# Windowed attention into a gated feed-forward on one core: w_in's casts shared with ScalarE, and units 4 to 15 at other places in the order

## The chip, the core and the metric

The kernel runs on one core of one Trainium2 chip. The core has a matrix engine (TensorE, PE in the profile), VectorE (DVE), ScalarE (ACT), GpSimd (Pool, POOL) and a sync engine (SyncE, SP) that here only issues transfers. Each engine runs its own list of instructions in order, and they wait for each other by semaphores. Data come from HBM by DMA into SBUF; matmuls write to PSUM, of which this kernel uses all eight banks. The metric is the time of one execution on the device in microseconds (us). Three runs of the kernel before took 225.61, 227.72 and 227.89 us, a median of 227.72.

## The reference

q, k and v have 4 batches, 8 heads, 768 positions and 64 columns. A position attends to itself, the 127 before it and the first four positions ("sinks"). The outputs of the heads side by side are x, 3072 tokens by 512, and x goes through two matrix products with a gate between them.

```python
scores = q @ k.T / sqrt(64)                    # kept where key < 4 or 0 <= query - key < 128
x = softmax(scores) @ v                        # per head; heads joined: 3072 x 512
h = x @ w_in                                   # 512 x 2048
g = h * (1 / (1 + exp(-beta * h)))
out = g @ w_out                                # 2048 x 512, float32
```

## The kernel before

**Units and tiles.** The attention is done in 32 units. Unit n is one pair of heads (n % 4) of one batch (n // 8) and one half of the sequence, 384 positions (n // 4 % 2). Four units fill one tile T = n // 4 of 384 tokens of xT, the transposed x in bf16, one of four products' depth (c, 0 to 3) each. For T there are 16 tiles of h (128 columns of w_in by 384 tokens): tile i is T = i // 16, m = i % 16. Each is four matmuls (c = 0 to 3, `hidden_matmul`), a tanh on ScalarE (`tanh`, line 755) and the gate on VectorE (`gate`, line 769), which multiplies the tanh plus one by h in place of the logistic function (the 0.5 goes into the output copy, beta is halved) and leaves g in bf16. Then 3 x 16 projections of g against w_out per T (`project`, line 796) accumulate the output rows, which ScalarE or VectorE copies out.

**A unit's steps** are named "in", "sink", "a", "b", "av" and "out". "in" (`transpose_in`, line 513) turns q and k with six 128-column transposes on TensorE into one PSUM bank, and one copy (line 522) takes them to qkT. "a" and "b" (`scores`, line 569) are two chunks of scores with an exponential on ScalarE after each (line 576); then VectorE multiplies the result by a 0/1 mask (`mask`, line 587). For units in ADDED (n < 6) the mask is put in otherwise: two 384-column matmuls by the identity (line 561) add a large negative number to the masked scores in PSUM first, and the VectorE product is left out. "sink" is the score against the four sink keys, for units of the second half only (units 4 to 7 among these). "av" (`attend`, line 696) multiplies by v, `normalise` divides by the sum (lines 705 and 707), and "out" (`transpose_out`, line 724) turns the result into xT, with a copy at line 728. From unit 12 on the transposes are done by DMA, and two chunks go as one.

**Loads and casts.** All inputs arrive in float32. `load(n)` fetches q, k and v of a unit (590 KB), `load_w(i)` one of eight pieces of w_in (i < 8) or of w_out (512 KB each), all on SyncE's queue in the order of the calls. Piece i of w_in holds 512 of its columns and two of the four depths: tiles m = 0 to 3 need pieces 0 and 1, m = 4 to 7 pieces 2 and 3, m = 8 to 11 pieces 4 and 5, m = 12 to 15 pieces 6 and 7; the even piece serves c = 0 and 1, the odd one c = 2 and 3. Pool casts each piece to bf16 (`cast_w`, line 478, 128 x 1024), and q, k and v of each unit (`cast`, lines 490 and 493), into three buffers for q and k that units take in turn.

**PSUM.** `six` is six banks: s0, s1, tr and av (scores, transposes, attention output) and h0 and h1. Two more are acc0 and acc1. Tiles 0 to 3 use acc0, acc1, h1 and h0; tiles 4 to 15 only acc0 and acc1 in turn; tiles 16 to 31 all four; later tiles others. Before the first tile is gated, TensorE is also given matmuls on constants (`keep_busy`).

**The order.** The body writes operations down by slots s. Slot s = 0 to 31 holds tile i = s; 32 to 47 the projections of T = 0; from 48 on tile s - 16 with the projections of the T before. EARLY gives units 4 to 7 their slots by step, as fractions between tiles; FIRST gives units 8 to 31 their slot of "in", with "sink", "a", "b", "av", "out" 1, 2, 3, 5 and 7 slots later. BANK_B and BANK_S choose the PSUM banks of units 4 to 7. `loads` and `casts` tie later loads and casts to slots. This is not yet the order of execution: `Prog.order` simulates the five engines and the DMA queues with the written costs (`busy`, `lag`; transfers by size over a rate) and places, engine by engine, whichever ready operation can start first within a window of 160. Its result is a fixed list for each engine, so an operation whose input arrives later than planned holds up those behind it.

Of the kernel before, what the change touches and what calls it, by code (L numbers as in the profile page):

```python
# [17 lines left out]
TT = 384  # L18
# [5 lines left out]
NW = 8  # L24
# [17 lines left out]

EARLY = {4: {'in': 0.2, 'sink': 3.0, 'a': 3.4, 'b': 5.0, 'av': 5.6, 'out': 8.0},
# [244 lines left out]
def bass_streamingllm_window__then__act_swish_beta_kernel(  # L288
# [187 lines left out]
    def cast_w(i):  # L476
        view, _, dst = w_piece(i)
        op("gp", lambda e: e.tensor_copy(dst, view), r=[("wst", i % NW)],  # L478
           w=[("w_in" if i < NW else "w_out", i % NW)], busy=985.0, lag=100.0)

    def cast(n, first=False):
        _, _, half, pb = place(n)
        z = n % NQK

        def view(name):
            return stage[name][pb][:, :, 3 * half:3 * half + 3, :].rearrange("p h c d -> p c h d")

        for x, name in enumerate("qk"):
            eng = "dve" if first and name == "k" else "gp"
            op(eng, lambda e, x=x, name=name: e.tensor_copy(qk16[z][:, x, :, :, :], view(name)),  # L490
               r=[(name + "_stage", pb, half, hh) for hh in range(2)], w=[(name + "16", z)],
               busy=451.0, lag=100.0)
        op("gp", lambda e: e.tensor_copy(v_aug[pb][:, 3 * half:3 * half + 3, :, 0:D], view("v")),  # L493
           r=[("v_stage", pb, half, hh) for hh in range(2)], w=[("v_aug", pb, half)], busy=451.0,
           lag=100.0)
# [56 lines left out]
    def scores(n, c, bank, name):  # L552
        _, _, half, pb = place(n)
        at = 0
        if n < ADDED:
            w = width(half, c)
# [7 lines left out]
        with P.together("pe"):  # L564
            for kb, qb, nq in CHUNKS[half][c]:
                w = 128 * nq
                for hh in range(2):
                    rows = slice(64 * hh, 64 * hh + 64)
                    op("pe", lambda e, at=at, w=w, kb=kb, qb=qb, hh=hh, rows=rows: e.matmul(  # L569
                        bank[:, hh, at:at + w], qkT[pb][rows, kb // 3, 1, kb % 3 * 128:kb % 3 * 128 + 128],  # L570
                        qkT[pb][rows, half, 0, qb % 3 * 128:qb % 3 * 128 + w], start=n >= ADDED,
                        stop=True, skip_group_check=n < ADDED),
                       r=[("qT", pb, half), ("qkT", pb, kb // 3)], w=[f"{name}{hh}"],
# [6 lines left out]
    def mask(n, c):  # L580
        if n < ADDED:
            return
# [161 lines left out]
    def hidden_matmul(i, c):  # L744
# [28 lines left out]
    def project_last(half, m):  # L773
# [4 lines left out]
                                           w_out16[:, m, cols], start=(m == 0), stop=(m == NM - 1)),  # L778
                  r=[("g", T % 2, m), ("w_out", m // 2)], w=[name], **pe(256))
        if m == NM - 1:  # L780
# [14 lines left out]
    def project(T, t, m, bank, name, eng="act"):  # L795
        node = op("pe", lambda e: e.matmul(bank, g[T % 2][:, m, t * 128:(t + 1) * 128],  # L796
                                    w_out16[:, m, :], start=(m == 0), stop=(m == NM - 1)),
           r=[("g", T % 2, m), ("w_out", m // 2)], w=[name], **pe(NOUT))
        if m == NM - 1:
# [33 lines left out]
    for hh in range(2):  # L833
# [15 lines left out]
    load_w(7)  # L849
# [66 lines left out]
    for s in sorted(slots):  # L916
# [14 lines left out]
        for n, step in here:  # L931
            half = place(n)[2]
            if step == "in" and n < XBAR:
                transpose_in(n, eng="dve")
            if step == "sink" and half == 1:
                scores_sink(n, *((h_ps[:, 0, :], "h0") if BANK_S.get(n) == "h" else (s_ps[:, 0, :], "s0") if n < PAIRED
                                 else (tr_ps, "tr")))
# [17 lines left out]
            if step == "out":  # L955
                if n < XBAR:
                    transpose_out(n, eng="act" if n < 8 else "dve")
        if s in casts:
# [102 lines left out]
```

## Time and profile before

| what | value |
|---|---|
| median of three runs | 227.72 us |
| the profiled execution | 226.35 us |
| its span, first to last instruction | 224.6 us |
| granted TensorE clock | 1.000 |
| TensorE busy | 216.6 us (96%) |
| ScalarE busy | 142.0 us |
| VectorE busy | 133.3 us |
| Pool busy | 75.2 us |
| first projection of T = 0 starts | 51.53 us |

The profile is of one execution; its own time is 1.75 us longer than its span. Times inside it count from the first instruction. A matmul row is counted from its start to its modelled end, and rows overlap, so a row's mean is longer than the distance between matmuls that follow each other. In rows of the order of time, "x8" says that eight instructions were merged, and brackets tell how long the engine had been idle and what ended that. In groups, the columns are the operation with its shapes, the count, busy time and mean ns of one, then idle time of the engine ahead of it.

### The profile page before, as it was taken

To read this page: it belongs to the slowest core of one execution; us is meant where nothing else is said; L and a number is where in the kernel's file an instruction comes from. 1 tells how busy PE (TensorE), PEld (TensorE's weight loads), DVE (VectorE), ACT (ScalarE), POOL (GpSimd) and SP (SyncE) were. 2 spreads that over 40 slices of the span, in tenths; PEclk is the share of its full clock that TensorE was granted. 3 is DMA by queue.
4 is the path that set the end of the run, shared out by engine and by line. 5 is a ranking of instruction groups with operands and counts; after the bars stand their busy time and mean duration, and the time that the engine had idled before them with its cause. 6 is when DMAs were issued, how large, how long until landed. Compare 5 with 4: busy or idle time off the path is not lost.

```text
span 224.6 us, 4507 instructions
## 1 busy us (share of the span) xinstructions
PE 216.6 (96%) x1732; PEld 122.5 (55%) x1753; DVE 133.3 (59%) x259; ACT 142.0 (63%) x222; POOL 75.2 (33%) x149
## 2 busy tenths in 40 slices
PE   7997999999999999999999999999999999999995
PEld 4463555655555555555465655555556565555554
DVE  5477787897766535555285566667667666254300
ACT  2674897794446666556587669566877584465410
POOL 6769569599335211444301623700000000000000
PEclk9999999999999999999999999999999999999999
DMA  6999999899999899999998999551021002111012
GB/s 186 292 330 287 270 339 288 270 392 278 142 206 221 241 229 167 277 260 190 235 238 184 227 223 182 146 136 32 32 85 64 20 9 72 50 47 47 22 74 95
DMA packets 95438, 39.80 MB, mean 177 GB/s; under 512 B 81960, under 2 KB 88376, under 8 KB 95416
## 3 DMA queue, kind: packets, MB, share of 16 engines
q1 hardware_dynamic: 93760, 38.75, 69.3%
q10 hardware_dynamic: 1656, 0.76, 1.2%
q8 instruction: 14, 0.23, 0.4%
q14 instruction: 8, 0.07, 0.1%
HBM read 27.30 MB, written 6.29 MB: 150 GB/s over the span
## 4 chain that ended last, share of the span: by engine, by line
PE 89%; DVE 4%; DMA 2%; ACT 1%; issue 1%; POOL 0%; ACTq 0%; DVEq 0%
PE acc L796 34%; PE six L747 30%; PE acc L747 6%; PE six L696 5%; PE six L642 3%; DMA v_stage<-in_v_dram 2%; PE six L569 2%; PE six L796 1%; PE six L513 1%; PE six L685 1%; PE six L542 1%; DVE g L769 1%; PE six L561 1%; DVE v_sink L891 1%; DVE qkT L522 1%
## 5 line engine op out<-in xcount | busy, mean ns | idle before, releaser
L796 PE MATMUL acc<-w_out,g 128*128 128x512 bf16 x332 | 84.4, 379 | 0.9
L755 ACT ACTIVATE th<-six,beta_half 128x384 f32<-128x384 f32 x106 | 61.1, 582 | 30.5 <-PE six L747 25.2
L747 PE MATMUL six<-xT,w_in 128*128 128x384 bf16 x424 | 78.1, 326 | 0.1
L769 DVE SCALAR_TENSOR_TENSOR g<-th,six 128x384 bf16<-128x384 f32 x106 | 57.2, 551 | 28.9 <-ACT th L755 25.9
L747 PEld LDWEIGHTS six<-xT,w_in 128*128 128x128 bf16 x424 | 40.4, 98 | 29.1 <-ACT E L613 0.7
L796 PEld LDWEIGHTS acc<-w_out,g 128*128 128x128 bf16 x352 | 32.9, 98 | 33.9 <-issue 1.8
L662 DVE TENSOR_TENSOR E<-E,mask_all 128x1536 bf16<-128x1536 bf16 x20 | 19.4, 972 | 30.1 <-ACT E L654 24.8
L654 ACT ACTIVATE E<-six 128x1536 bf16<-128x1536 f32 x16 | 22.3, 1448 | 10.6 <-PE six L642 10.6
L490 POOL CAST qk<-q_stage 128x384 bf16<-128x384 f32 x32 | 17.7, 554 | 29.8 <-DMA q_stage<-in_q_dram 17.0
L576 ACT ACTIVATE E<-six 128x768 bf16<-128x768 f32 x24 | 18.8, 810 | 9.3 <-PE six L569 9.3
L493 POOL CAST v_aug<-v_stage 128x384 bf16<-128x384 f32 x32 | 16.7, 532 | 16.2 <-DMA v_stage<-in_v_dram 9.6
L490 POOL CAST qk<-k_stage 128x384 bf16<-128x384 f32 x31 | 16.5, 532 | 16.3 <-DMA k_stage<-in_k_dram 16.2
L804 ACT ACTIVATE out_sb<-acc 128x512 f32<-128x512 f32 x22 | 12.9, 598 | 12.4 <-PE acc L796 12.2
L696 PEld LDWEIGHTS six<-v_aug,E 128*128 128x128 bf16 x384 | 17.0, 97 | 4.3 <-POOL v_aug L493 0.7
L696 PE MATMUL six<-v_aug,E 128*128 128x65 bf16 x384 | 18.9, 193 | 0.5 <-POOL v_aug L493 0.3
L707 DVE TENSOR_TENSOR o_norm<-six,rden 128x384 bf16<-128x384 f32 x32 | 17.8, 557 | 1.4
L747 PE MATMUL acc<-xT,w_in 128*128 128x384 bf16 x88 | 16.8, 327 | 1.2 <-DVE g L769 1.2
L755 ACT ACTIVATE th<-acc,beta_half 128x384 f32<-128x384 f32 x22 | 12.7, 583 | 5.6 <-PE acc L747 4.9
L769 DVE SCALAR_TENSOR_TENSOR g<-th,acc 128x384 bf16<-128x384 f32 x22 | 11.7, 551 | 3.7 <-ACT th L755 3.3
L747 PEld LDWEIGHTS acc<-xT,w_in 128*128 128x128 bf16 x88 | 7.9, 98 | 7.0 <-DVE g L769 2.1
L478 POOL CAST w_in<-wst 128x1024 bf16<-128x1024 f32 x8 | 9.0, 1129 | 6.1 <-DMA wst<-in_moe_w_in_dram 5.8
L522 DVE COPY qkT<-six 128x768 bf16<-128x768 bf16 (+1 forms) x10 | 9.1, 913 | 2.4 <-PE six L513 2.4
(72 smaller groups left out, 156.7 us busy)
## 6 DMA issues: line engine op xcount, KB each, us to landing
out_dram<-out_sb SPq DMA_DIRECT2D x23, 256.0 KB, 2.6
wst<-in_moe_w_in_dram SPq DMA_DIRECT2D x8, 512.0 KB, 6.4
wst<-in_moe_w_out_dram SPq DMA_DIRECT2D x8, 512.0 KB, 7.7
q_stage<-in_q_dram SPq DMA_DIRECT2D x8, 384.0 KB, 4.2
k_stage<-in_k_dram SPq DMA_DIRECT2D x8, 384.0 KB, 3.9
v_stage<-in_v_dram SPq DMA_DIRECT2D x8, 384.0 KB, 4.0
v_stage<-in_v_dram SPq DMA_DIRECT2D x30, 96.0 KB, 3.9
q_stage<-in_q_dram SPq DMA_DIRECT2D x12, 192.0 KB, 5.0
```

The lines of the kernel that those rows point to most:

```text
L490: op(eng, lambda e, x=x, name=name: e.tensor_copy(qk16[z][:, x, :, :, :], view(name)), r=[(name + "_stage", pb, half, hh) for hh in range( ...
L493: op("gp", lambda e: e.tensor_copy(v_aug[pb][:, 3 * half:3 * half + 3, :, 0:D], view("v")), r=[("v_stage", pb, half, hh) for hh in range(2 ...
L576: op("act", lambda e: e.activation(E[n % 2][:, c, :, 0:at], bank[:, 0:2, 0:at], AF.Exp, bias=0.0, scale=SCALE), x=[f"{name}0", f"{name}1"] ...
L654: op("act", lambda e, u=u, first=first: e.activation(E[u % 2][:, :, :, :].rearrange("p c h x -> p (c h x)"), six[:, first:first + 3, :].re ...
L662: op("dve", lambda e: e.tensor_tensor(both, both, mask_all[:, half, :].unsqueeze(1).to_broadcast([128, 2, 768]), ALU.mult), r=[("E", z, 0) ...
L696: last=(x == len(kbs) - 1): e.matmul(av_ps[:, at + hh * D1:at + hh * D1 + D1], E[z][:, c, h2, col:col + 128], v_aug[pb][:, kb, hh, :], sta ...
L707: op("dve", lambda e: e.tensor_tensor(o_norm[o][:, :, :, :].rearrange("p m h d -> p (m h) d"), src[:, :, 0:D], rden[z][:, :].unsqueeze(2). ...
L747: return op("pe", lambda e: e.matmul(bank, w_in16[:, c, m * 128:(m + 1) * 128], xT[:, c, T * TT:(T + 1) * TT], start=(c == 0), stop=(c == 3)),
L755: op("act", lambda e: e.activation(th[i % 3][:, :], bank, AF.Tanh, bias=0.0, scale=beta_half[:, m:m + 1]), x=[name], r=["beta"], w=[("th", ...
L769: op("dve", lambda e: e.scalar_tensor_tensor(g[T % 2][:, m, :], th[i % 3][:, :], 1.0, bank, ALU.add, ALU.mult), r=[("th", i % 3)], x=[name ...
L796: node = op("pe", lambda e: e.matmul(bank, g[T % 2][:, m, t * 128:(t + 1) * 128], w_out16[:, m, :], start=(m == 0), stop=(m == NM - 1)), r ...
L804: op("act", lambda e: e.activation(out_sb[z][:, :], bank, AF.Copy, bias=0.0, scale=0.5), x=[name], w=[("out_sb", z)], **act(NOUT))
```

## The change

Five things change, all in the order and in who does which cast; what is computed is the same.

- `cast_w`: pieces 1, 2, 3 and 5 of w_in are cast in two halves, one depth by Pool and one by ScalarE (128 x 512 each). The tiles' products wait for their own depth (`w_in` has a third index).
- `hidden`: tiles 4 to 19 issue their four products as four separate operations, so that the planner can put other work between them or start one before the others' inputs are there.
- Loads: unit 4 is loaded after piece 0 and unit 5 after piece 2; unit 6 comes ahead of pieces 4 and 5, and unit 7 after them.
- The set ADDED: chunk a of unit 6 and chunk b of unit 7 take their mask by matmuls too; `mask` leaves VectorE's product out for them.
- Slots and engines of units 4 to 31: EARLY, FIRST, banks; ScalarE copies the transposes in for units 4 and 9 and out for units 6 and 7, VectorE the others of units 4 to 11 (before: VectorE all in, ScalarE out for units 4 to 7). Some written costs (985 to 1080 ns for a piece, 451 to 530 ns for a cast of q, k or v) and the slots of later loads change with them.

```diff
-EARLY = {4: {'in': 0.2, 'sink': 3.0, 'a': 3.4, 'b': 5.0, 'av': 5.6, 'out': 8.0},
-         5: {'in': 2.4, 'sink': 3.8, 'a': 3.8, 'b': 6.6, 'av': 6.8, 'out': 9.6},
-         6: {'in': 3.9, 'sink': 6.9, 'a': 7.0, 'b': 8.0, 'av': 14.7, 'out': 15.0},
-         7: {'in': 6.9, 'sink': 13.2, 'a': 13.2, 'b': 14.0, 'av': 14.8, 'out': 15.7}}
-BANK_B = {4: 'h', 5: 's', 6: 'h', 7: 's'}
-BANK_S = {4: 'h', 5: 'h', 6: 'h', 7: 'h'}
-
-FIRST = {8: 27, 9: 33, 10: 34, 11: 38}
-FIRST.update({12: 44, 13: 47, 14: 50, 15: 53, 16: 60, 17: 60})
-FIRST.update({n: 68 + 8 * (n // 2 - 9) for n in range(18, NU)})
+EARLY = {4: {'in': -3.3, 'sink': 3.1, 'a': -3.0, 'b': 1.5, 'av': 3.2, 'out': 5.8},
+         5: {'in': -0.7, 'sink': 5.1, 'a': 4.0, 'b': 5.7, 'av': 9.3, 'out': 13.3},
+         6: {'in': 3.3, 'sink': 8.0, 'a': 7.2, 'b': 8.5, 'av': 12.7, 'out': 14.6},
+         7: {'in': 5.6, 'sink': 12.0, 'a': 9.3, 'b': 12.5, 'av': 12.8, 'out': 15.4}}
+BANK_B = {4: 's', 5: 'h', 6: 'h', 7: 'h'}
+BANK_S = {4: 't', 5: 'h', 6: 'h', 7: 't'}
+
+TURN_IN = {4: 'act', 5: 'dve', 6: 'dve', 7: 'dve', 8: 'dve', 9: 'act', 10: 'dve', 11: 'dve'}
+TURN_OUT = {4: 'dve', 5: 'dve', 6: 'act', 7: 'act', 8: 'dve', 9: 'dve', 10: 'dve', 11: 'dve'}
+
+APART = 20
+
+HALVED = (1, 2, 3, 5)
+
+FIRST = {8: 17, 9: 23, 10: 27, 11: 28}
+FIRST.update({12: 39, 13: 43, 14: 46, 15: 50, 16: 60, 17: 60})
+FIRST.update({n: (68, 76, 83, 92, 99, 108, 116)[n // 2 - 9] for n in range(18, NU)})
...
-ADDED, FAR = 6, -float(1 << 20)
+ADDED = {*((n, c) for n in range(4) for c in range(2)), (4, 0), (4, 1), (5, 0), (5, 1), (6, 0), (7, 1)}
+FAR = -float(1 << 20)
...
     def cast_w(i):
         view, _, dst = w_piece(i)
+        name = "w_in" if i < NW else "w_out"
+        if i in HALVED:
+            n = 1
+            op("act", lambda e: e.copy(dst[:, n:], view[:, n:]), r=[("wst", i % NW)], w=[(name, i % NW, 1)],
+               **act(512))
+            op("gp", lambda e: e.tensor_copy(dst[:, 0:n], view[:, 0:n]), r=[("wst", i % NW)],
+               w=[(name, i % NW, 0)], busy=600.0, lag=100.0)
+            return
         op("gp", lambda e: e.tensor_copy(dst, view), r=[("wst", i % NW)],
-           w=[("w_in" if i < NW else "w_out", i % NW)], busy=985.0, lag=100.0)
+           w=[(name, i % NW, 0), (name, i % NW, 1)], busy=1080.0, lag=100.0)
...
-           r=[("w_in", m // 4 * 2 + c // 2), ("xT", T, c)], w=[name], **pe(TT))
+           r=[("w_in", m // 4 * 2 + c // 2, c % 2), ("xT", T, c)], w=[name], **pe(TT))
...
     def hidden(i):
-        with P.together("pe"):
-            for c in range(3 if i < 4 else 0, 4):
-                node = hidden_matmul(i, c)
+        for cs in ((3,),) if i < 4 else ((0,), (1,), (2,), (3,)) if i < APART else (range(4),):
+            with P.together("pe"):
+                for c in cs:
+                    node = hidden_matmul(i, c)
         tanh(i)
         return node
...
     load_w(0)
+    load(4)
     load_w(1)
     load_w(2)
+    load(5)
     load_w(3)
-    load(4)
-    load(5)
     load(6)
-    load(7)
     load_w(4)
     load_w(5)
+    load(7)
     load_w(6)
     load_w(7)
...
-    at = {16: 38, 17: 46, 18: 52, 19: 57, 24: 69, 25: 75, 26: 81, 27: 87}
+    at = {16: 38, 17: 44, 18: 50, 19: 55, 24: 70, 25: 76, 26: 84, 27: 89}
```

More of the change, by code (lines that the diff above doesn't have):

```diff
@@ L491, in cast @@
                r=[(name + "_stage", pb, half, hh) for hh in range(2)], w=[(name + "16", z)],
-               busy=451.0, lag=100.0)
+               busy=530.0, lag=100.0)
         op("gp", lambda e: e.tensor_copy(v_aug[pb][:, 3 * half:3 * half + 3, :, 0:D], view("v")),
-           r=[("v_stage", pb, half, hh) for hh in range(2)], w=[("v_aug", pb, half)], busy=451.0,
+           r=[("v_stage", pb, half, hh) for hh in range(2)], w=[("v_aug", pb, half)], busy=530.0,
            lag=100.0)
@@ L554, in scores @@
         at = 0
-        if n < ADDED:
+        if (n, c) in ADDED:
             w = width(half, c)
@@ L570, in scores @@
                         bank[:, hh, at:at + w], qkT[pb][rows, kb // 3, 1, kb % 3 * 128:kb % 3 * 128 + 128],
-                        qkT[pb][rows, half, 0, qb % 3 * 128:qb % 3 * 128 + w], start=n >= ADDED,
-                        stop=True, skip_group_check=n < ADDED),
+                        qkT[pb][rows, half, 0, qb % 3 * 128:qb % 3 * 128 + w], start=(n, c) not in ADDED,
+                        stop=True, skip_group_check=(n, c) in ADDED),
                        r=[("qT", pb, half), ("qkT", pb, kb // 3)], w=[f"{name}{hh}"],
@@ L580, in mask @@
     def mask(n, c):
-        if n < ADDED:
+        if (n, c) in ADDED:
             return
@@ L778, in project_last @@
                                            w_out16[:, m, cols], start=(m == 0), stop=(m == NM - 1)),
-                  r=[("g", T % 2, m), ("w_out", m // 2)], w=[name], **pe(256))
+                  r=[("g", T % 2, m), ("w_out", m // 2, m % 2)], w=[name], **pe(256))
         if m == NM - 1:
@@ L797, in project @@
                                     w_out16[:, m, :], start=(m == 0), stop=(m == NM - 1)),
-           r=[("g", T % 2, m), ("w_out", m // 2)], w=[name], **pe(NOUT))
+           r=[("g", T % 2, m), ("w_out", m // 2, m % 2)], w=[name], **pe(NOUT))
         if m == NM - 1:
@@ L933, in bass_streamingllm_window__then__act_swish_beta_kernel @@
             if step == "in" and n < XBAR:
-                transpose_in(n, eng="dve")
+                transpose_in(n, eng=TURN_IN.get(n, "dve"))
             if step == "sink" and half == 1:
-                scores_sink(n, *((h_ps[:, 0, :], "h0") if BANK_S.get(n) == "h" else (s_ps[:, 0, :], "s0") if n < PAIRED
+                scores_sink(n, *((h_ps[:, 0, :], "h0") if BANK_S.get(n) == "h" else (tr_ps, "tr") if BANK_S.get(n) == "t" else (s_ps[:, 0, :], "s0") if n < PAIRED
                                  else (tr_ps, "tr")))
@@ L956, in bass_streamingllm_window__then__act_swish_beta_kernel @@
                 if n < XBAR:
-                    transpose_out(n, eng="act" if n < 8 else "dve")
+                    transpose_out(n, eng=TURN_OUT.get(n, "dve"))
         if s in casts:
```

## The prediction, made before the changed kernel was run

> **What bounds the kernel now.** I read the page first, then the windows by stage, then the order of time where the windows show holes.
>
> ```profile
> span 224.6 us, 4507 instructions
> PE 216.6 (96%) x1732; PEld 122.5 (55%) x1753; DVE 133.3 (59%) x259; ACT 142.0 (63%) x222; POOL 75.2 (33%) x149
> DMA  6999999899999899999998999551021002111012
> ```
>
> TensorE is busy 96% of the span, and the DMA engines are full from 5 to about 150 us. The change lies in the first 70 us. Its stages, by the windows (after the times: length, then busy us and instructions of each engine, clock, DMA share, GB/s):
>
> ```profile
> 18.30:31.00 12.70, 11.01 (x121) 6.13 (x119) 9.63 (x18) 10.30 (x18) 9.03 (x17) 1.00 0.97 293
> 31.00:41.00 10.00, 9.60 (x88) 5.79 (x87) 7.74 (x16) 8.06 (x16) 7.21 (x12) 1.00 1.01 289
> 41.00:51.20 10.20, 10.20 (x81) 6.07 (x79) 9.61 (x18) 9.12 (x17) 9.08 (x14) 1.00 0.99 348
> 51.20:66.50 15.30, 15.05 (x134) 7.66 (x133) 10.82 (x23) 6.14 (x9) 8.90 (x17) 1.00 0.99 202
> 66.50:225.00 158.50, 154.46 (x1166) 87.25 (x1183) 84.59 (x158) 98.89 (x150) 28.49 (x59) 1.00 0.60 136
> ```
>
> Busy time flatters TensorE, since a lone matmul also counts its drain. So I price its work by rows of the chain that stand back to back: eight x @ w_in products (128x384) 1.30 us, three projections 0.65, twelve attention products 0.36, three transposes 0.17, a score chunk 0.27 and 0.11 for the change into it. Times the counts of the groups in each window this is 10.8 us of work in the 12.7 us from 18.3; 9.25 of 10.0; about 10.2 of 10.2; 14.9 of 15.3. So **TensorE loses 1.9 + 0.75 us between 18.3 and 41 us and nearly nothing from there to 66.5**. Before 18.3, from the first transposes at 4.5, it has about 11 us of work in 13.8. What makes the holes, in order of time (start, length, instruction, in brackets the idle time and what ended it):
>
> ```profile
> 28.96 1.04 POOL L478 CAST w_in<-wst 128x1024 bf16<-128x1024 f32 x1 [2.61 <-DMA wst<-in_moe_w_in_dram]
> 30.31 1.16 POOL L478 CAST w_in<-wst 128x1024 bf16<-128x1024 f32 x1 [0.31 <-DMA wst<-in_moe_w_in_dram]
> 31.52 0.76 PEld L747 LDWEIGHTS acc<-xT,w_in 128*128 128x128 bf16 x6 [0.38 <-POOL w_in L478]
> ...
> 33.77 1.04 POOL L478 CAST w_in<-wst 128x1024 bf16<-128x1024 f32 x1 [0.38 <-PE six L696]
> ```
>
> ```profile
> 37.21 1.21 DVE L769 SCALAR_TENSOR_TENSOR g<-th,acc 128x384 bf16<-128x384 f32 x2 [0.26 <-ACT th L755]
> 37.83 1.47 PE L747 MATMUL acc<-xT,w_in 128*128 128x384 bf16 x8 [0.40 <-DVE g L769]
> ```
>
> Pieces 4 and 5 of w_in land at 29 and 30.3 us, so tiles 8 and 9 wait until 31; between 25 and 31 no tile runs. From there the pairs of tiles, 10 and 11 to 14 and 15, follow at 33.59, 35.74 and 37.83: two accumulators, each held for product, tanh and gate, give a pair every 2.1 us, and TensorE waits for the gate.
>
> **The loads.** From w_in 0 (cast at 13.73) to w_in 7 (33.77) 20.0 us bring seven pieces (0.524 MB) and four units (0.590 MB): 301 GB/s, 1.74 us a piece, 1.96 a unit. Estimated by these, pieces 1 to 7 land at 15.4, 17.2, 18.9, 28.5, 30.3, 32.0, 33.7 before, within 0.5 us of their casts in the trace. The new order gives: unit 4 15.7, w1 17.4, w2 19.1, unit 5 21.1, w3 22.8, unit 6 24.8, w4 26.5, w5 28.3, unit 7 30.2, w6 32.0, w7 33.7. Unit 4 gains 5 us, pieces 4 and 5 gain 2, pieces 1 to 3 lose 2 to 4, unit 7 loses 3.4, the last piece is where it was: no byte is saved. Nothing else is passed on SP's queue; loads from unit 8 on stand behind the same bytes.
>
> **The halved casts.** Pool's half is taken as half of 1.04 = 0.52; ScalarE's, 512 columns, as 0.55 (its copy of 384 columns is 0.47, its 512-column out_sb is 0.60): a piece is ready 0.5 us sooner, Pool is spared 2.1 us, ScalarE gets 2.2. Bounds: nothing gained, to 0.5 us on each. The copies on ScalarE add waits for a landing; behind each are queued exponentials and tanhs.
>
> **Tiles product by product.** Tiles 4 to 19 issue the same matmuls; a tile can start on piece 2 while piece 3 is on its way, and tiles 18 and 19 on finished units while unit 7 is not. Cost at nothing: successive products load new weights anyway (98 ns under a 163 ns product).
>
> **Tiles, worked forward.** Tiles 4 and 5 start at 20.5 as before, but end at 24.0 with w3 (22.8 + 0.55 + two products of each) and not at 22.3. Gates end at 25.2 and 25.7, tiles 6 and 7 at 26.5, 8 and 9 with w5's cast (28.9) and 0.65 at 29.6, 10 and 11 at about 31.8, 12 and 13 with w7's (34.8) at 35.5, 14 and 15 start at 36.4. In the trace they start at 37.83: **1.4 us**. By then units 4 to 7 must be through too. Unit 7 lands at 30.2; its output came 12 us after its v landed (25.84 to 37.73) in queues, while its shortest chain, cast 1.5, transposes and copy 1.5, scores and exps 2, products, normalising and output 2, is 7: 37 us, just in time. Tiles 18 and 19 can have up to three of four products done by then (6 x 0.163 = 1.0). So 1.4 to 2.4 us; I take **2.3**, the holes being 2.65 and unit 4's early work also fitting in the hole before 18.3.
>
> **Masks as matmuls.** Chunks (6, a) and (7, b) get two more 384-column products each: 4 x 0.163 = 0.65 us of TensorE; VectorE loses two masks of 0.56 to 0.73. They lie in the holes of 25 to 34; without that cover they cost 0.65. I take **0.2**.
>
> **Units 8 to 15 earlier.** Unit 8 goes from tile 27 to 17, 9 from 33 to 23, 10 and 11 to 27 and 28; its data was cast by 36.5 in the trace and its transposes ran at 41.7, so it is ready. Nothing is saved; 4.0 us of TensorE work (a unit of these: transposes 0.34, scores 0.76, products 0.36, output 0.17) moves out of the projections of tile 0 into x @ w_in of tile 1. There it needs other engines: through tile 31 ScalarE gets six exps of 0.81, two copies of unit 4's and 9's transposes at about 0.81 (the exp has their shape), the halves 2.2, and loses two outputs of 0.47: 27.5 + 7.7 = 35.2 us. VectorE gets 5.7 on 27.0. TensorE's work to there is 30.5 + 4.65 = 35.2 us. **ScalarE has as much to do as TensorE**; in the same stage of the trace it was 89% and VectorE 94% busy. What relieves it: the exps of units 10 and 11 (3.2 us) may come after the last tanh, the projections leaving ScalarE idle 9 of 15.3 us. I take **0.3** lost; the bounds are 0 and rival 2's price. Units 12 to 15, loads 17 to 27: a few tiles, in stages where TensorE has no hole; 0, bounds 0.5 either way.
>
> The masks of units 8 to 11 move among w_out's casts on Pool. In the trace one such mask beside Pool's cast took 0.77 (at 49.70) and a free one 0.55. The Trainium skill (SBUF — State Buffer, Who interferes with whom) says that a VectorE instruction with two SBUF inputs and a GpSimd one that reads SBUF exclude each other for a whole instruction; by that each could wait out a cast of 1.04, eight of them 8 us of VectorE. The rows bear out a part of it, 0.2 each.
>
> **Sum:** -2.3 + 0.2 + 0.3 = -1.8, and 0.2 for Pool's relief between 15 and 25 us (4.87 and 4.56 of 5 busy there): -2.0. The profiled execution took 226.35 us, 1.75 more than its span; so **224.3**. The three runs shown have a median of 227.72, 1.4 above that execution, and spread over 1%; about 1% (2.3 us) is what a measurement of this kernel can tell from no change.
>
> **Rivals.**
> 1. *The whole of the holes is filled.* 2.65 and 1 us ahead of 18.3, units 12 to 15 another 0.5: 222.3. For it: unit 4 five us earlier. Against it: w7 as late as ever, and two accumulators.
> 2. *ScalarE becomes the bound in x @ w_in of tile 1: slower.* Place: from 18.3 to tile 31. If its 35.2 us run at the 89% of 41 to 51.2, tile 31 ends at 18.3 + 39.5 = 57.8; left then are 14.9 - 4.0 and the 0.4 lost in the stage, 11.3: 69.1 in place of 66.5, **229.0**. It decides when ScalarE can't keep 95% (36.9 us: 55.2 + 11.3 = 66.5). For it: VectorE's 32.7 us beside it. Against it: exps that may slide.
> 3. *The early gain is eaten.* A copy of w_in stands at ScalarE's head before its piece has landed. The planner counts 380 GB/s where 301 are had, so it can be wrong by a transfer, 1.74 us, with tanhs and exps behind it, whose banks TensorE waits for; or unit 7, 3.4 us later, takes the place of the weights. Either gives back 1.7: **226.1**. For it: tiles 4 and 5 do end later. Against: TensorE has units 4 to 6 meanwhile.
>
> **Chances:** the forecast 0.38 (223.3 to 225.3), rival 1 0.18, rival 3 0.22, rival 2 0.22. Of the forecast's case a little over half lies past 1%: faster 0.40, same 0.38, slower 0.22. The range takes rival 1 to 221.5 and rival 2 up to its price.
>
> **What would show it.** Right: w_in 4's first product by 28 us; tile 14's first product near 36.4; ScalarE's four 512-column copies of 0.55 with idle under 0.5 us before each; projections beginning near 53 and their stage 2 to 4 us shorter than 15.3. Wrong: ScalarE waiting over 1 us for a load; TensorE idle between 40 and 55 on gates or exps; units 8 to 11 still last among the projections; loads of w_in 7 later than 34.

## The result

The changed kernel takes 225.21 us (median of 15 runs, 224.74 to 227.08) against 226.75 us of the kernel before, run 15 times beside it (225.61 to 227.89). The ratio is **0.9945, 95% interval 0.9925 to 0.9965**: 1.25 us quicker (0.8 to 1.7), a clear gain but of little more than half a per cent. The forecast was 2.0 us quicker. The direction was right, the size is 0.6 of it. The ratio of the two medians alone would be 0.9932; it lies inside the same interval.

The page of the changed kernel, the lines that answer to those of before. Line numbers have moved: x @ w_in is now line 763 (was 747), the tanh 771 (755), the gate 786 (769), the projection 813 (796), the mask matmuls 577 (561), the score chunks 585 (569).

```profile
span 223.6 us, 4498 instructions
PE 216.8 (97%) x1736; PEld 122.4 (55%) x1757; DVE 129.3 (58%) x257; ACT 143.3 (64%) x226; POOL 74.0 (33%) x149
DMA  6999998996789999999999899862020202111012
```

TensorE does as much as before in a span that is 1.0 us shorter; VectorE has 4 us less, ScalarE 1.3 us more. The windows by stage of the changed kernel (after the times: length, then busy us and instructions of TensorE, its weight loads, VectorE, ScalarE and Pool, clock, DMA share, GB/s):

```profile
18.30:31.00 12.70, 12.12 (x121) 6.56 (x121) 7.62 (x14) 11.53 (x22) 8.27 (x14) 1.00 1.10 360
31.00:41.00 10.00, 10.00 (x105) 6.31 (x102) 8.95 (x20) 8.00 (x15) 7.29 (x13) 1.00 0.88 251
41.00:51.20 10.20, 10.20 (x87) 5.92 (x85) 9.74 (x20) 9.88 (x19) 9.26 (x15) 1.00 1.05 367
51.20:66.50 15.30, 15.14 (x123) 7.56 (x125) 9.92 (x21) 7.03 (x11) 8.41 (x15) 1.00 0.70 155
```

Two things are to be seen. TensorE has no idle left between 25 and 51 us (10.00 of 10.00, 10.20 of 10.20). And the transfers of the first stage run at 360 GB/s where the kernel before had 293; they are not the same transfers, though, since the order of the loads puts other ones into this window. Priced by work, as the prediction did (the same prices, the counts of the groups), TensorE does 22.15 us of work between 18.3 and 41 us instead of 20.43, so **1.72 us more; 0.65 of it are the added mask matmuls, and the progress is 1.07 us**. (Each sum is of three windows, 18.3 to 25, 25 to 31 and 31 to 41, and a matmul across a border is in two of them. Counted in one window from 18.3 to 41 it is 21.56 against 19.92, 1.64 us more.) From 41 to 66.5 both kernels do the same, 25.6 us after the change and 25.4 before. The gain of the span, 1.0 us, is there at 41 us and is kept to the end.

These two profiles do not start level: w_in's first piece is cast at 12.81 us in the changed kernel and at 13.73 in the kernel before. One of the kernels below ("exponentials of units 8 to 11 short") has the changed kernel's order and differs from it only from about 41 us on, and in its profile, of the slowest of its twelve executions, the first piece is cast at 13.79. It does 20.84 us of work in the one window, 0.92 more than before, and its span is 224.2 us, 0.4 shorter. So a good part of the 1.64 us seems to hang on when the pieces landed in the execution that was profiled: with the first pieces level, the filled holes are some 0.9 us, masks included. The 1.25 us of the runs do not depend on the two profiles.

In order of time, w_in's last piece and the last pair of tiles of T = 0 in the changed kernel (start, length, instruction, idle time and its end in brackets):

```profile
31.40 1.04 POOL L494 CAST w_in<-wst 128x1024 bf16<-128x1024 f32 x1 [1.29 <-DMA wst<-in_moe_w_in_dram]
```

```profile
34.59 1.48 PE L763 MATMUL acc<-xT,w_in 128*128 128x384 bf16 x8
36.77 0.81 PE L763 MATMUL acc<-xT,w_in 128*128 128x384 bf16 x4
```

The last piece is cast at 31.40 instead of 33.77. Tiles 12 and 13 are the eight products at 34.59, tile 14 starts at 36.77, where it started at 37.83 before and the prediction had 36.4. The hole that remains is ahead of 25 us: 1.1 us by work between 18.3 and 25, of 1.35 before. The chain of the changed kernel there (start, length, what):

```profile
19.46 0.80 ACT qkT L538
20.26 0.95 ACT th L771 x2
21.21 0.70 ACT E L592
21.91 0.94 ACT th L771 x2
22.86 0.51 ACT w_in L489
23.36 0.72 ACT E L592
24.09 0.05 issue
24.13 0.50 PE six L577 x2
```

From 19.46 to 24.09 the chain is ScalarE's in one piece of 4.6 us: the copy of unit 4's transposes that the change gave it, the tanhs of tiles 0 to 3 behind it (the first at 20.16 instead of 19.22), two exponentials, and its half of w_in 3.

### The profile page after: what moved, and what is told of

Its sections match the earlier page's. It is cut to its first block, busy times and chain, and to the rows that moved or that the text cites. A ratio compares the mean times of both kernels' runs of the same rounds, so it can differ in the third digit from the quotient of the medians.

```text
span 223.6 us, 4498 instructions
## 1 busy us (share of the span) xinstructions
PE 216.8 (97%) x1736; PEld 122.4 (55%) x1757; DVE 129.3 (58%) x257; ACT 143.3 (64%) x226; POOL 74.0 (33%) x149
## 4 chain that ended last, share of the span: by engine, by line
PE 88%; SPq 4%; DMA 3%; ACT 2%; issue 1%; POOL 0%; DVE 0%; DVEq 0%
PE acc L813 34%; PE six L763 31%; PE acc L763 6%; PE six L712 5%; DMA wst<-in_moe_w_in_dram 3%; PE six L658 3%; SPq L455 2%; SPq L447 2%; PE six L585 2%; PE six L813 2%; PE six L701 1%; PE six L529 1%; PE six L558 1%; ACT th L771 1%; PE six L794 1%
## 5 line engine op out<-in xcount | busy, mean ns | idle before, releaser
L763 PE MATMUL six<-xT,w_in 128*128 128x384 bf16 x424 | 79.5, 326 | 0.1
L786 DVE SCALAR_TENSOR_TENSOR g<-th,six 128x384 bf16<-128x384 f32 x106 | 56.5, 550 | 26.5 <-ACT th L771 24.8
L813 PEld LDWEIGHTS acc<-w_out,g 128*128 128x128 bf16 x352 | 32.7, 98 | 33.8 <-issue 1.8
L678 DVE TENSOR_TENSOR E<-E,mask_all 128x1536 bf16<-128x1536 bf16 x20 | 19.6, 980 | 35.7 <-ACT E L670 26.4
L506 POOL CAST qk<-q_stage 128x384 bf16<-128x384 f32 x32 | 17.2, 536 | 26.9 <-DMA q_stage<-in_q_dram 16.2
L509 POOL CAST v_aug<-v_stage 128x384 bf16<-128x384 f32 x32 | 17.3, 552 | 21.1 <-DMA v_stage<-in_v_dram 16.0
L592 ACT ACTIVATE E<-six 128x768 bf16<-128x768 f32 x24 | 19.3, 818 | 5.7 <-PE six L585 5.7
L763 PE MATMUL acc<-xT,w_in 128*128 128x384 bf16 x88 | 18.5, 327 | 0.7 <-POOL w_in L491 0.4
L723 DVE TENSOR_TENSOR o_norm<-six,rden 128x384 bf16<-128x384 f32 x32 | 17.8, 557 | 1.2
L561 ACT ACTIVATE E_sink<-six 128x384 bf16<-128x384 f32 x16 | 7.9, 497 | 5.7 <-PE six L558 5.7
L763 PEld LDWEIGHTS acc<-xT,w_in 128*128 128x128 bf16 x88 | 7.4, 98 | 5.4 <-DVE g L786 0.8
L701 PE MATMUL six<-v_sink,E_sink 128*128 128x130 bf16 x48 | 9.2, 220 | 0.1
```

What stands on the lines that cost most here:

```text
L592: op("act", lambda e: e.activation(E[n % 2][:, c, :, 0:at], bank[:, 0:2, 0:at], AF.Exp, bias=0.0, scale=SCALE), x=[f"{name}0", f"{name}1"] ...
L678: op("dve", lambda e: e.tensor_tensor(both, both, mask_all[:, half, :].unsqueeze(1).to_broadcast([128, 2, 768]), ALU.mult), r=[("E", z, 0) ...
L723: op("dve", lambda e: e.tensor_tensor(o_norm[o][:, :, :, :].rearrange("p m h d -> p (m h) d"), src[:, :, 0:D], rden[z][:, :].unsqueeze(2). ...
L763: return op("pe", lambda e: e.matmul(bank, w_in16[:, c, m * 128:(m + 1) * 128], xT[:, c, T * TT:(T + 1) * TT], start=(c == 0), stop=(c == 3)),
L786: op("dve", lambda e: e.scalar_tensor_tensor(g[T % 2][:, m, :], th[i % 3][:, :], 1.0, bank, ALU.add, ALU.mult), r=[("th", i % 3)], x=[name ...
```

## The experiments

Each ratio is to the kernel before, run on the same chip; the change itself is at 0.9945 (0.9925 to 0.9965), measured in a run of its own. The kernel before had medians of 226.75 us beside the change and of 226.36, 226.35 and 226.17 beside the experiments. The difference of two such ratios is uncertain by about 0.003 (0.6 to 0.7 us). Where the planner makes a new order, an experiment undoes its part and everything that the planner hangs on it; three kernels keep the order of the changed kernel instruction by instruction (the mask matmuls and the exponentials below).

| kernel | order | ratio to before, 95% | w_in's first and last cast, us |
|---|---|---|---|
| before | | 1 | 13.73, 33.77 |
| the change | | 0.9945 (0.9925 to 0.9965) | 12.81, 31.40 |
| old order of loads | new | 1.0031 (1.0012 to 1.0049) | 13.52, 33.27 |
| before with the new loads alone | new | 1.0103 (1.0063 to 1.0142) | 13.29, 31.56 |
| casts whole | new | 0.9978 (0.9958 to 0.9999) | 13.12, 30.95 |
| two masks on VectorE | new | 1.0086 (1.0053 to 1.0119) | 13.07, 32.72 |
| the two masks' matmuls short | kept | 0.9953 (0.9933 to 0.9973) | 13.61, 32.07 |
| unit 4 copied in by VectorE | nearly kept | 0.9971 (0.9944 to 0.9998) | 13.48, 32.60 |
| products together | new | 1.0017 (0.9993 to 1.0041) | 13.16, 31.18 |
| old slots of units 8 to 31 | new | 0.9987 (0.9962 to 1.0011) | 12.85, 31.63 |
| the two masks' matmuls three times | kept | 1.0016 (0.9992 to 1.0040) | 12.96, 31.26 |
| exponentials of units 8 to 11 short | kept | 0.9957 (0.9937 to 0.9977) | 13.79, 32.45 |
| tiles 20 to 31 product by product too | new | 0.9986 (0.9956 to 1.0016) | 12.82, 30.97 |
| piece 7 halved too | new | 1.0049 (1.0026 to 1.0072) | 12.99, 31.16 |

### The order of the loads, undone and alone

```diff
 # in the changed kernel: back to the old order
     load_w(0)
-    load(4)
     load_w(1)
     load_w(2)
-    load(5)
     load_w(3)
+    load(4)
+    load(5)
     load(6)
+    load(7)
     load_w(4)
     load_w(5)
-    load(7)
     load_w(6)
     load_w(7)
```

> The change with one thing undone: the loads again in the order of before (pieces 0 to 3 of w_in, units 4 to 7, pieces 4 to 7). Theory A, the order of the loads is what makes the early gain, and it also makes the transfers themselves quicker, since large-packet pieces now stand between small-packet units: the last piece of w_in is cast near 33.8 us again (31.4 in the changed kernel), TensorE again lacks work between 20 and 31 us, and the time is that of before or slower, ratio 1.00 to 1.01. Theory B, the places of the steps and the separate products make the gain, and the quicker transfers of the changed kernel's profile were chance: the last piece is cast near 31.4 and the ratio stays near 0.995.

> The kernel before with the new order of the loads and nothing else. Theory A: the last piece of w_in is cast near 31.4 us instead of 33.8, tiles 8 and 9 run near 28.5 instead of 31.0, but unit 7 comes 3 us later; a part of the gain, ratio 0.996 to 1.000. Theory B: the last piece stays near 33.8 and the ratio is 1.000 to 1.005, because units 5 and 7 come at other times than the old places expect.

Measured: 1.0031 with the loads undone, 1.0103 with the loads alone in the kernel before. Theory A holds for the transfers. The windows from 15 to 31 us, one line for each kernel, the last number GB/s: before, the change, the change with old loads, before with new loads.

```profile
15.00:31.00 16.00, 14.10 (x154) 8.08 (x154) 12.57 (x23) 11.83 (x21) 12.19 (x21) 1.00 0.98 303
```

```profile
15.00:31.00 16.00, 14.93 (x150) 8.16 (x148) 10.04 (x19) 13.65 (x26) 10.72 (x20) 1.00 1.09 354
```

```profile
15.00:31.00 16.00, 13.77 (x142) 7.51 (x140) 9.75 (x18) 12.59 (x23) 10.11 (x21) 1.00 1.01 307
```

```profile
15.00:31.00 16.00, 13.24 (x130) 7.51 (x129) 9.74 (x18) 10.22 (x19) 12.27 (x22) 1.00 1.05 340
```

303 and 307 GB/s in the old order, 354 and 340 in the new one. The windows do not hold the same transfers, and from 31 to 41 us it is the other way round (289 GB/s before, 251 in the change). The same bytes are those from w_in 0 to w_in 7, seven pieces and four units, 6.03 MB in either order. In the old order w_in 7 is cast 20.0 and 19.8 us after w_in 0, which is 301 and 305 GB/s; in the twelve kernels with the new order 17.8 to 19.7 us after it, 338 to 307 GB/s, and in the changed kernel 18.6 us, 324 GB/s. So the new order is quicker in every one of them, by 8% in the changed kernel; of the 2.4 us by which its last piece comes sooner, 0.9 are its earlier first piece.

Theory A is wrong on the time of the loads alone: they make the kernel before 1% slower, although the last piece comes 2 us sooner. A part is lost early: with pieces 1 to 3 later, TensorE does 4.36 us of work from 18.3 to 25 instead of 5.35, and makes up 0.45 of that by 31. The window behind that and its chain show the rest:

```profile
31.00:41.00 10.00, 8.97 (x99) 4.84 (x95) 8.90 (x19) 8.04 (x16) 7.08 (x12) 1.00 0.94 273
```

```profile
31.85 0.81 ACT E L576
32.66 0.37 ACT xT L728
33.03 0.71 ACT E L576
33.75 0.37 ACT xT L728
34.12 0.39 ACT E_sink L545
34.52 0.47 ACT th L755
34.98 0.71 ACT E L576
```

From 31.85 to 35.7 the chain is ScalarE's, exponentials, outputs and a tanh in one row: TensorE does 8.28 us of work in these 10 us instead of 9.26. That unit 7, which comes later, crowds there with unit 6 at the old places is the likely reason; no run tried it. So the new order of loads is worth 0.9% to the changed kernel and costs 1% without the rest: **the loads and the places of the units' steps are one edit**.

### The halved casts

```diff
-HALVED = (1, 2, 3, 5)
+HALVED = ()
```

> The change with HALVED empty: all pieces of w_in cast whole by Pool. Theory C, the halved casts cost more than they bring: ScalarE is 5.00 of 5 us busy from 20 to 25 us in the changed kernel, and its copies push the first tanh from 19.2 to 20.2 us; then without them the first tanh is back near 19.3 and the ratio to before is 0.991 to 0.994. Theory D, the half us by which a piece is ready sooner is worth more: ratio 0.996 to 0.999.

Measured: 0.9978, 0.0033 above the change (0.75 us), by intervals that overlap a little. Theory C falls: the first tanh is at 20.26 without the copies too, so they don't push it. Theory D has the better of it, though this order is a new one as well, and a part of the 0.75 us may be the order's.

### The two masks as matmuls

```diff
-ADDED = {*((n, c) for n in range(4) for c in range(2)), (4, 0), (4, 1), (5, 0), (5, 1), (6, 0), (7, 1)}
+ADDED = {*((n, c) for n in range(4) for c in range(2)), (4, 0), (4, 1), (5, 0), (5, 1)}
```

> The change with chunk (6, a) and chunk (7, b) masked by VectorE again: four 384-column matmuls fewer, 0.65 us of TensorE, and two masks of 0.56 to 0.8 us more on VectorE. Theory E, the holes of 25 to 41 us are filled in the changed kernel (no slack by work), so the matmuls are paid in full: 0.4 to 0.65 us quicker than the change, ratio to before 0.991 to 0.993. Theory F, VectorE (4.96 of 5 us busy from 30 to 35) would be the bound without them: ratio 0.995 to 0.998.

Measured: 1.0086. Neither theory had that: 0.65 us of TensorE's work less, and 3 us slower than the change. But the planner made another order (the lists of all five engines differ from the change's), w_in 7 is cast at 32.72, and TensorE has only 8.95 us of work in the 10 us from 31 to 41. So this run prices an order and not the masks. The next two keep the order:

```diff
 # the masks short: 32 columns, and the scores start their banks anew
-  bank[:, hh, 0:w], ident[:, :], far[:, first:first + w], start=True, stop=False,
+  bank[:, hh, 0:32 if n > 5 else w], ident[:, :], far[:, first:first + (32 if n > 5 else w)], start=True, stop=n > 5,
...
-  start=(n, c) not in ADDED,
+  start=(n, c) not in ADDED or n > 5,
```

> The change with the same order on every engine, instruction by instruction; only the four mask matmuls of chunks (6, a) and (7, b) are 32 columns wide instead of 384, and the scores behind them start their banks anew. So the mask of these two chunks is left out (beyond their scores nothing is computed differently). It takes away 4 x 352 columns, about 0.59 us of TensorE, and nothing else. Theory E, TensorE has no slack there and the masks are paid in full: 0.5 to 0.6 us quicker than the change, ratio to before 0.991 to 0.993. Theory G, TensorE waits for something else right behind them: ratio 0.994 to 0.996.

```diff
 # the masks three times
-  op("pe", lambda e, hh=hh, w=w: e.matmul(
-      bank[:, hh, 0:w], ident[:, :], far[:, first:first + w], start=True, stop=False, skip_group_check=True),
+  op("pe", lambda e, hh=hh, w=w: [e.matmul(bank[:, hh, 0:w], ident[:, :], far[:, first:first + w],
+      start=True, stop=False, skip_group_check=True) for _ in range(3 if n > 5 else 1)][-1],
```

> The change with the same order on every engine; only each of the four mask matmuls of chunks (6, a) and (7, b) is issued three times (the last one counts, the result is the same). It adds eight 384-column matmuls, 1.30 us of TensorE between 27 and 34 us. Theory E, TensorE has no slack from there on: ratio to before 0.999 to 1.001, that is 0.005 to 0.006 above the change. Theory G, TensorE stands there in the lee of something later, as the unchanged time of the short masks suggests: ratio 0.994 to 0.997. In between, the first 0.5 to 0.7 us is hidden and the rest is paid: 0.997 to 0.999.

Measured: 0.9953 for the short masks, 1.0016 for the triple ones. Three times the masks cost 0.0071 over the change, 1.6 us (with an uncertainty of 0.7) for 1.30 us of matmuls: paid in full. Short masks bring nothing that can be measured (0.0008 above the change, where 0.0026 below it was expected). TensorE's order of time around them, in the triple and in the short kernel:

```profile
27.26 1.14 PE L577 MATMUL six<-far_b,ident 128*128 128x384 bf16 x6
28.33 0.34 PE L585 MATMUL six<-qkT 64*128 64x128 bf16 x4
...
32.67 1.14 PE L577 MATMUL six<-far_b,ident 128*128 128x384 bf16 x6
33.65 0.81 PE L763 MATMUL acc<-xT,w_in 128*128 128x384 bf16 x4
```

```profile
28.25 0.20 PE L577 MATMUL six<-far_b,ident 128*128 128x32 bf16 x2
28.39 0.34 PE L585 MATMUL six<-qkT 64*128 64x128 bf16 x4
...
32.73 0.20 PE L577 MATMUL six<-far_b,ident 128*128 128x32 bf16 x2
32.92 0.82 PE L763 MATMUL acc<-xT,w_in 128*128 128x384 bf16 x4
```

In the changed kernel the same products start at 32.81. The triple kernel is 0.46 us ahead of it at 25.3 us and 0.84 behind at 33.65, which is 1.3 in all, and still 0.76 behind at the first projection (52.50 against 51.74). The short kernel is 0.54 us behind at 26.2 and only 0.11 at 32.9, so the short masks do save 0.43 in place; but it had started late, with w_in's first cast at 13.61 instead of 12.81, and is 0.21 behind at the first projection. That accounts for the profiled execution. Why twelve runs show no gain either stays open; with an uncertainty of about 0.003, the difference of +0.0008 all but reaches the -0.0026 that was expected.

### Unit 4's copy

```diff
-TURN_IN = {4: 'act', 5: 'dve', ...
+TURN_IN = {4: 'dve', 5: 'dve', ...
```

> The change with unit 4's transposes copied by VectorE instead of ScalarE; the order is otherwise nearly the same (Pool and SyncE unchanged). Theory H, the hole left at 18 to 25 us (1.1 us by work) is ScalarE's, which is 5.00 of 5 us busy from 20 to 25 and starts the first tanh at 20.16, while VectorE idles 2.5 us for it: the first tanh at about 19.4, tile 4 at about 20.6 instead of 21.4, and 0.3 to 0.7 us gained, ratio to before 0.991 to 0.993. Theory I, the hole is set by the landing of w_in 3 and unit 5: ratio 0.994 to 0.996.

Measured: 0.9971 (0.9944 to 0.9998). No gain from 0.8 us less on ScalarE's chain ahead of the first tanh, so theory H in this form falls. In its profile w_in 1 and 3 are cast at 18.09 and 22.28 (17.60 and 21.62 in the change), and TensorE does 5.2 us of work between 18.3 and 25 instead of 5.6; so it has to be read from the cast of w_in 1 on. Counted from there the first tanh does come sooner, 2.03 us after it instead of 2.56:

```profile
20.12 1.05 ACT L771 ACTIVATE th<-acc,beta_half 128x384 f32<-128x384 f32 x2 [0.16 <-PE acc L763]
```

But now it waits for TensorE's product (the bracket), and unit 4's first product with v (line 701, the sink keys) comes 7.16 us after that cast instead of 7.24. The hole ahead of 25 us has ScalarE's chain, TensorE's products behind w_in 1 and the landings near each other; relieving the one did not fill it.

### Products together, and the old slots

```diff
-APART = 20
+APART = 4
```

> The change with APART = 4: the four products of each of tiles 4 to 19 are one operation again; the planner makes another order from there. Theory J, separate products fill the holes: tile 4 starts only with w_in 3 (about 22.4 us), the work done by 41 us is 0.5 to 1 us less, ratio to before 0.997 to 1.001. Theory K, two accumulators set the pace anyway: ratio 0.994 to 0.996.

Measured: 1.0017, 0.0072 above the change (1.6 us). Theory J holds: tile 4's first product is at 22.82, behind w_in 3, instead of 21.38, and TensorE does 20.96 us of work between 18.3 and 41 instead of 22.15 (both as sums of three windows). The order is a new one, so the 1.6 us are the price of the four products together with that order.

```diff
-FIRST = {8: 17, 9: 23, 10: 27, 11: 28}
-FIRST.update({12: 39, 13: 43, 14: 46, 15: 50, 16: 60, 17: 60})
-FIRST.update({n: (68, 76, 83, 92, 99, 108, 116)[n // 2 - 9] for n in range(18, NU)})
+FIRST = {8: 27, 9: 33, 10: 34, 11: 38}
+FIRST.update({12: 44, 13: 47, 14: 50, 15: 53, 16: 60, 17: 60})
+FIRST.update({n: 68 + 8 * (n // 2 - 9) for n in range(18, NU)})
...
-    at = {16: 38, 17: 44, 18: 50, 19: 55, 24: 70, 25: 76, 26: 84, 27: 89}
+    at = {16: 38, 17: 46, 18: 52, 19: 57, 24: 69, 25: 75, 26: 81, 27: 87}
```

> The change with units 8 to 31 and the later loads at the slots of before; the planner makes another order. Theory L, moving units 8 to 15 saves nothing: ratio to before 0.993 to 0.996. Theory M, with the holes ahead of 41 us filled by tiles of T = 0, the tiles of T = 1 need the units' work among them to keep TensorE busy: ratio 0.997 to 1.001. Rival 2 of the prediction (ScalarE, 9.88 of 10.2 us busy from 41 to 51.2, holds up TensorE): ratio below 0.993.

Measured: 0.9987, 0.0042 above the change (0.9 us), with intervals that almost touch. Nearer to theory M than to L, and rival 2 would have shown the other sign. The edit moves units 8 to 31 and the later loads at once, and the order is new, so it does not price units 8 to 15 alone. The profile does not show where: the work done by 66.5 us is the same 46.6 us, and its span is 0.3 us longer, all of it later.

### ScalarE among the tiles of T = 1

```diff
-  op("act", lambda e: e.activation(E[n % 2][:, c, :, 0:at], bank[:, 0:2, 0:at], AF.Exp,
+  op("act", lambda e, u=128 if 7 < n < 12 else at: e.activation(E[n % 2][:, c, :, 0:u], bank[:, 0:2, 0:u], AF.Exp,
```

> The change with the same order on every engine; only the eight exponentials of units 8 to 11 are taken over 128 of each head's 384 columns, so two thirds of these units' softmax weights are not computed (old values of the buffer stand in their place). It takes 8 x 0.43 = 3.4 us from ScalarE between 42 and 58 us. Rival 2 of the prediction, ScalarE paces TensorE among the tiles of T = 1: ratio to before 0.985 to 0.991. The forecast's term of 0.3 us: ratio 0.992 to 0.994. TensorE does not wait for ScalarE there at all: ratio 0.994 to 0.996.

Measured: 0.9957. The window of this kernel:

```profile
41.00:51.20 10.20, 10.20 (x86) 5.90 (x86) 9.97 (x20) 8.56 (x19) 9.26 (x14) 1.00 1.05 376
```

ScalarE has 8.56 us to do where the change has 9.88, TensorE is full in both, and the time is that of the change. TensorE does not wait for ScalarE there: at the load that ScalarE has in the changed kernel, rival 2's mechanism is not at work.

### Two tries at a better version

```diff
 # one:
-APART = 20
+APART = 32
 # the other:
-HALVED = (1, 2, 3, 5)
+HALVED = (1, 2, 3, 5, 7)
```

> The change with APART = 32: tiles 20 to 31 product by product too; the planner makes another order. A try at a better version. If separate products help wherever units' work is mixed with tiles: ratio to before 0.990 to 0.993. If they only help where weights or x come late (tiles 4 to 19): ratio 0.994 to 0.997.

> The change with piece 7 of w_in halved too; the planner makes another order. A try at a better version. Piece 7 is the last one and is ready 0.4 us sooner; ScalarE has 0.6 us more at 31 us, where it is 8.0 of 10 us busy. If the last piece holds up tiles 12 to 15: ratio to before 0.991 to 0.993. If the accumulators do: ratio 0.994 to 0.997.

Measured: 0.9986 and 1.0049. The second is worse than the change and outside what either reading allowed. The first (0.9956 to 1.0016) is no better than the change and, by intervals that overlap, probably worse; of its two readings it is nearer to the second. In the first, with tiles 20 to 31 apart too, TensorE's progress to 41 us is as good as the change's, but projections begin at 53.69 instead of 51.74, and from 51.2 to 66.5 TensorE is busy 14.62 us instead of 15.14. In the second TensorE loses 0.4 us of busy time from 31 to 41 and 0.3 from 41 to 51.2, and projections begin at 54.76. No version beat the change.

## Why the prediction was right in its direction, and wrong in its terms

**The holes (2.3 us): right mechanism, a quarter too large or more.** The gain is in work filled into the holes between 18.3 and 41 us, as forecast, and is kept to the end; measured 1.72 us in the two profiles, and 0.9 in the pair whose first pieces of w_in come at the same time. What was missed is the hole ahead of 25 us, which I let unit 4's early work fill. 1.1 of 1.35 us stayed, and the chain there is ScalarE's for 4.6 us: the copies that the change gives ScalarE were counted as work (2.2 and 0.8 us) and not as a place in its queue. Neither relief of ScalarE that I tried gained anything, so what would fill that hole is open.

**The loads: a wrong step that cost little.** "The last piece is where it was: no byte is saved" is wrong. The bytes are the same, but they come 8% quicker in the new order (18.6 us for 20.0), and the last piece lands 2.4 us sooner, 0.9 of it because the first one did. The step took the mean rate of one order for that of another. The planner, whose rate was called too high in rival 3, was nearer: it counts 380 GB/s for pieces only, 300 for q and k and 235 for v, which makes 18.2 us for these eleven loads. The mistake mattered little. From 25 us on TensorE has no idle, and the chain from 25.5 to 41 is TensorE's alone, so neither a late piece nor an accumulator holds it up there. Tile 8, forecast for 28 us at the latest, has its first product at 28.41 with its weights cast at 25.75, and tile 14 starts at 36.77, with TensorE at other work until then. That tile 14 came near the forecast 36.4, which was worked out from a last piece cast at 34.8, is therefore luck.

**The halved casts (about 0), and Pool's relief (0.2).** Sizes: 0.62 us on ScalarE and 0.61 on Pool, not 0.55 and 0.52. The Trainium skill (ScalarE: Activation LUTs, What ACT_TABLE_LOAD costs) gives 186 ns and 0.833 ns for each column where scale and bias are immediate; the estimate by it is 612 ns for 512 columns. The trace's 607 to 654 ns agree, and so would the row of 512 columns that I had, out_sb at 0.60; I took less. Halves and relief together were undone in one run, which puts their worth at some 0.75 us with an uncertainty of 0.65 and another order in it: more than the 0.2 of the forecast, but not by a clear margin.

**The separate products: the step that I priced least.** They stand in the prediction as a way for the holes to fill; undone, they take back 1.6 us (uncertain by 0.7), more than the whole gain. Together with the loads (2.0 us when undone), the halves (0.75) and the slots (0.9) the parts sum to over 5 us, while the change is worth 1.25. They are not terms of a sum. Each undone run also has an order of its own, so these prices can't be added; that each part holds the others up is shown for the loads and the places alone (0.9% with them, -1% without).

**The masks (0.2): mis-sized.** I let the holes of 25 to 34 us cover two thirds. There is no hole there any more in the changed kernel, and the triple kernel pays each matmul in full: 0.65 us is their price. The short kernel, which should then have gained, did not, so the price is shown for adding and not for taking away.

**ScalarE and VectorE in T = 1 (0.3) and rival 2: wrong, 0.** The step that failed is the move itself. By the first projection (51.53 and 51.74) the changed kernel has transposed three of units 8 to 11 instead of two, scored two instead of one, attended one as before and turned one out instead of none: 1.3 us of TensorE's work by the same prices, not 4.0. So from 18.3 to 51.2 ScalarE has 29.4 us to do (27.5 before), not 35.2, and VectorE 26.3, not 32.7; projections begin at 51.74 and not near 53, and 45 of them lie between 51.2 and 66.5 as before. Rival 2's load was never there. Where ScalarE is full all the same, 97% from 41 to 51.2 (9.88 of 10.2) with VectorE at 95%, TensorE still has every instruction in time, so busy shares were also the wrong measure. The likely reason is that with four accumulators TensorE has something else to do while one is being gated; no run tried fewer.

The masks among Pool's casts did grow longer: four of them took 0.94, 0.70, 0.81 and 0.97 us instead of 0.55. Two of them with the cast that was running when they began:

```profile
48.29 1.04 POOL L494 CAST w_out<-wst 128x1024 bf16<-128x1024 f32 x1
48.93 0.81 DVE L603 TENSOR_TENSOR E<-E,mask_a 128x768 bf16<-128x768 bf16 x1
```

```profile
50.97 1.04 POOL L494 CAST w_out<-wst 128x1024 bf16<-128x1024 f32 x1 [0.28 <-DMA wst<-in_moe_w_out_dram]
51.46 0.97 DVE L603 TENSOR_TENSOR E<-E,mask_b 128x768 bf16<-128x768 bf16 x1
```

All four end 0.40 to 0.42 us after the end of that cast, however early they began: the mask waits until Pool's instruction is through. That is the exclusive lock that the Trainium skill states (SBUF — State Buffer, Who interferes with whom), and the trace agrees with it in full. The prediction's 0.2 for each was no partial lock but the rest of a cast that was already under way; a mask loses more the earlier in a cast it begins. The profile shows nobody who waited for these masks.

**Units 8 to 15 earlier ("nothing is saved").** The run with the old slots takes back some 0.9 us, with an uncertainty of 0.7. It moves units 8 to 31 and the later loads back at once, in a new order, so which of them saves it, and where, stays open.

With the terms of the two profiles the sum is -1.72 + 0.65 + 0 = -1.07 us, and the runs say -1.25; with the first pieces level it is -0.92 + 0.65 = -0.27 in the profiles. Rival 1 (all holes filled) fell at the hole ahead of 25 us. Of rival 3 the one half, a copy of w_in at ScalarE's head waiting for its landing, shows with 1.06 and 0.50 us of idle before the first two copies, when ScalarE had nothing else (in the kernel with whole casts it idles 3.53 us there); the wait of over 1 us, named as a sign of being wrong, is there and cost nothing that the runs show. Ahead of the other two there was no idle.

## What to carry to other kernels

When the order of several engines is planned together, an edit's price from a run with a new order is the price of that order: taking 0.65 us of work away made this kernel 3 us slower. Keep the order fixed, and shrink or repeat the one instruction in place, to learn what its time costs. A full engine beside a full TensorE is no bound by its busy share; look for a wait behind it. And the sequence of transfers is also a matter of their rate, not of their order alone. Before two profiles are subtracted, look whether they start level: here two executions of one order, whose first pieces landed a microsecond apart, had done 0.7 us more and less work by 41 us.

## What the runs showed of the hardware that was not expected

The same six megabytes, from the first to the last piece of w_in, took 20.0 and 19.8 us (301 and 305 GB/s) when four units' loads stood together between two sets of w_in pieces, and 17.8 to 19.7 us (338 to 307 GB/s) in the twelve kernels in which pieces and units alternated, with the DMA engines full in all of them. By the kernel's addresses a piece is read in runs of 2 KB, q and k in runs of 768 bytes and v in runs of 256. That large and small packets share the engines better when mixed is argued, not shown; shown is that the time follows the order, in the kernel before and in the changed one alike, with a spread among kernels of the same order that nearly closes the gap.

The first piece of w_in, which stands in the same place in the queue of all fourteen kernels, was cast anywhere from 12.81 to 13.79 us, and both ends belong to kernels with one and the same order: a scatter of one microsecond, as large as the change's whole gain, that a single profile carries into every time behind it.

And a VectorE product of two SBUF tiles that begins during a Pool cast ends 0.40 to 0.42 us after the cast does, whether it was to wait 0.29 us for that (it took 0.70) or 0.55 (0.97). The other way round, Pool's cast of q that begins at 34.75 in the kernel before, during a mask, took 0.83 us instead of 0.51 and ended 0.36 after the mask.
